# First heads of a pair kept unnormalized: one reciprocal row and one broadcast per pair instead of one per head

## The chip, the cores and the metric

The kernel runs on one core of one Trainium2 chip. TensorE (PE) multiplies matrices into PSUM, VectorE (DVE), ScalarE (ACT) and GpSimd (POOL) work element by element, and SyncE (SP) issues the DMAs here. Each engine has its own list of instructions and waits on semaphores for the others. The metric is device time in microseconds (us): the median of the timed runs, beside one profiled execution whose trace is read. Line numbers such as L390 are those of the kernel before, unless a text says otherwise.

## The reference

One block with two halves, on 2048 rows of 576 columns: attention over cached keys and values, then a gated MLP. Both are framed by a layer norm and by shift, gain and gate from a conditioning vector. Cut to what the change touches:

```python
q = (x @ wq).reshape(B, Sq, 32, 128).transpose(0, 2, 1, 3)
k = jnp.repeat(k_cache[:, :, Sk - 512:, :], 2, axis=1)     # 16 key/value heads, each used by two query heads
v = jnp.repeat(v_cache[:, :, Sk - 512:, :], 2, axis=1)
scores = jnp.einsum("bhqd,bhkd->bhqk", q, k) * (128 ** -0.5)
p = softmax(scores, axis=-1)
o = jnp.einsum("bhqk,bhkd->bhqd", p, v)
attn = o.transpose(0, 2, 1, 3).reshape(B, Sq, 4096) @ wo
x = x + ga * attn
...
x = x + gb * ((silu(h @ w1) * (h @ w3)) @ w2)
```

Here `h` is the normed, shifted and scaled `x`. The softmax divides each row of `p` by its sum. That division can be made on `p`, on `o`, or, as long as all heads that are added up share a row's factor, on the product with `wo`.

## The kernel before

The kernel works in 32-bit precision out of 16-bit matmuls: an operand is split into a high f16 part and the f16 rest, and three products (high x high, high x low, low x high) are added in PSUM. Nearly every tensor is therefore made twice: a copy or cast for the high part, and a subtraction for the low part.

The rows stand in four blocks of 512 columns. Attention goes through 128 **slots**. A slot is one query head on one block; slots come in **pairs**, the two query heads (j = 0 and j = 1) of one key/value head on one block. The order of all engines' instructions is the order in which the main loop (L1465 to L1511) writes them: no scheduler moves anything. A slot i has four steps, t = 0 to 3, one per 128 rows. In slot i stand, on the way of one head:

- `query(i+1)` (L375), steps 0 to 2: fourteen matmuls into `pq`, a PSUM bank of tag "A"; at step 2 ACT writes the high half of `qT` (L384), and at step 3 `query_low` (L390, DVE) the low half. That is the last read of `pq`.
- `scores(i, t)` (L392): three matmuls into `pss` (tag "S"); DVE takes the row maximum (L404) and scales it (L405). The third matmul is the only one that reads the low half of `qT`.
- `weights(i, t)` (L417, ACT): the exponential `p`, and its row sums into a column of `l`.
- `half_high` and `half_low` (L449 ACT, L454 POOL), and a DMA transpose (L461) turn `p` for steps 0 to 2; step 3 of the slot before is turned by PE (L440), with its halves by ACT (L444) and DVE (L469).
- `sums(i-1, step)`: the reciprocals of `l` (L424, DVE) at step 0, the store of this row of 512 numbers to DRAM (L427) at step 1, and at step 2 its load back to all 128 partitions as `r` (L430), 256 KB.
- `values(i-1)` (L471), at the end of the slot: twelve matmuls into `po`, again a bank of tag "A".
- `normalize(i-2)` (L484) at step 1: DVE multiplies `po` by `r` into `on`. `split_on(i-2)` (L494) at step 3: ACT casts `on` to the high half of `o` (L498), POOL makes the low half (L499).
- `attend_out` (L501): six matmuls per 128 rows and head into `pe` (L353). The pair's two heads are added up in PSUM, then DVE adds the sum, times a factor of the key/value head, to `acc` (L507).

Tag "A" has two banks in all. A new tile of a tag takes the bank that was released first, and its first writer waits for the last reader of that bank.

Around this, the slots carry other work at fixed steps: the splitting of keys, values and weights, and the preparation of the MLP's weights. The MLP stage then follows (`mlp`, L907) with PE matmuls of its own (L764, L849).

Of the kernel before, what the change touches and what calls it, by code (L numbers as in the profile page):

```python
# [9 lines left out]
F32 = mybir.dt.float32  # L10
F32R = mybir.dt.float32r
F16 = mybir.dt.float16
I32 = mybir.dt.int32
AF = mybir.ActivationFunctionType
ALU = mybir.AluOpType
# [4 lines left out]
P = 128  # L20
# [4 lines left out]
SB = 512  # L25
NSB = S // SB
ST = SB // P
# [5 lines left out]
HALF = D // 2  # L33
# [6 lines left out]
SCALE = float(DH) ** -0.5  # L40
P_LOG = 15 * math.log(2.0)
Q_DOWN = 2.0**-17
EXPONENT = 0x7F800000


@with_exitstack
def tile_block(
# [13 lines left out]
    nc = tc.nc  # L61
# [3 lines left out]
    pool = ctx.enter_context(tc.tile_pool(name="pool", bufs=2))  # L65
    odd = ctx.enter_context(tc.tile_pool(name="odd", bufs=2))
# [7 lines left out]
    def bank(tag, name):  # L74
        return psum.tile([P, 512], F32, tag=tag, name=name)


    E = psum.tile([P, 2, 512], F32, tag="E", name="pe", bufs=1)
# [6 lines left out]
    def half_split(a):  # L85
        return a.rearrange("p (a n) -> p a n", a=2)
# [139 lines left out]
    factors = const.tile([P, HKV, 3], F32, name="factors")  # L226
    peaks = {}

    def powers(small, ps, lo, hi, n, down):

        d, up = small[:, n + lo : n + hi], small[:, 2 * n + lo : 2 * n + hi]
        nc.vector.tensor_scalar(d.bitcast(I32), ps[:, lo:hi].bitcast(I32), EXPONENT, None, op0=ALU.bitwise_and)
        nc.vector.tensor_scalar(d, d, 2.0**-40, down, op0=ALU.max, op1=ALU.mult)
# [114 lines left out]
    def back(o, w, t, first, last):  # L348

        rows = slice(t * P, (t + 1) * P)  # L350
        for n, (x, y) in enumerate(((0, 0), (0, 1), (1, 0))):
            for h in range(2):
                nc.tensor.matmul(  # L353
                    E[:, h, :HALF],
                    o[:, x, rows],
                    w[:, y, h * HALF : (h + 1) * HALF],
                    start=first and n == 0,
                    stop=last and n == 2,
                )
# [6 lines left out]
    uses = [(g, (p, p + 1), p == 0) for p in (0, 2) for g in range(FIRST)]  # L366
    uses += [(g, tuple(range(NSB)), True) for g in range(FIRST, HKV - TAIL)]
    uses += [(g, (p, p + 1), p == 0) for p in (0, 2) for g in range(HKV - TAIL, HKV)]
    slots = [(u, j, b) for u, (_, blocks, _) in enumerate(uses) for b in blocks for j in range(2)]
    begins = [next(i for i, slot in enumerate(slots) if slot[0] == u) for u in range(len(uses))]  # L370
    n = len(slots)
    state = [dict() for _ in range(n)]
    hT, wqs, keys, vals, wos = {}, {}, {}, {}, {}

    def query(i, part):  # L375
# [6 lines left out]
        if part == len(QP) - 1:  # L382
            q = st["qT"] = pool.tile([P, 2, SB], F16, tag=("qh", "ql")[i % 2], name="qT", bufs=QB)
            nc.scalar.activation(q[:, 0], ps, AF.Copy, scale=Q_DOWN)  # L384
            if not i:
                query_low(i)

    def query_low(i):
        q, ps = state[i]["qT"], state[i].pop("q")
        nc.vector.scalar_tensor_tensor(q[:, 1], ps, Q_DOWN, q[:, 0], op0=ALU.mult, op1=ALU.subtract)  # L390

# [16 lines left out]
    def weights(i, t):  # L408

        u, j, b = slots[i]  # L410
        factor = factors[:, uses[u][0], j : j + 1]
        st = state[i]
        pss, nm = st.pop(("max", t))
        if t == 0:
            st["l"] = odd.tile([P, 2 * ST], F32, tag="l", name="l", bufs=3)
        p = pool.tile([P, SB], F32, tag="p", name="p", bufs=PB)
        nc.scalar.activation(p, pss, AF.Exp, bias=nm[:, 1:2], scale=factor, accum_out=st["l"][:, t : t + 1])  # L417
        st["p", t] = p

    def sums(i, step):  # L420

        st = state[i]
        if step == 0:
            nc.vector.reciprocal(st["l"][:, ST:], st["l"][:, :ST])  # L424
        elif step == 1:
            st["row"] = dram.tile([P, ST], F32, name=f"row{i}")
            nc.sync.dma_start(st["row"], st["l"][:, ST:])  # L427
        elif step == 2:
            st["r"] = pool.tile([P, P, ST], F32, tag="kv", name="r", bufs=8)
            nc.sync.dma_start(  # L430
                st["r"].rearrange("d p t -> d (p t)"), st["row"].rearrange("p t -> (p t)").partition_broadcast(P)
            )
# [38 lines left out]
    def values(i):  # L471
# [9 lines left out]
                )  # L481
        st["po"] = po

    def normalize(i):  # L484
        st = state[i]
        po = st.pop("po")
        on = st["on"] = pool.tile([P, SB], F32, tag="raw", name="on", bufs=RB)
        nc.vector.tensor_mul(
            on.rearrange("d (t p) -> d t p", t=ST),
            po.rearrange("d (t p) -> d t p", t=ST),  # L490
            st["r"].rearrange("d p t -> d t p"),
        )

    def split_on(i):  # L494
        st = state[i]
        on = st.pop("on")
        o = st["o"] = pool.tile([P, 2, SB], F16, tag=("ah", "al")[i % 2], name="o", bufs=3)
        nc.scalar.copy(o[:, 0, :], on)  # L498
        nc.gpsimd.tensor_sub(o[:, 1, :], on, o[:, 0, :])  # L499

    def attend_out(pair, t, j, total):  # L501
        u, _, b = slots[2 * pair]
        back(state[2 * pair + j]["o"], wos[u][:, j], t, j == 0, j == 1)
        if j == 1:
            run(*total)
            a = half_split(acc[b][:, t, :])
            nc.vector.scalar_tensor_tensor(  # L507
                a, E[:, :, :HALF], factors[:, uses[u][0], 2:3], a, op0=ALU.mult, op1=ALU.add
            )


# [457 lines left out]
    def run(i, t):  # L969
        for task, args in tasks.pop((i, t), ()):  # L970
            task(*args)
# [20 lines left out]
    def scale_cols(kind, ps, small, down):  # L992

        nc.tensor.matmul(ps[:, :P], ones, spreads.pop(kind)[:, :P], start=True, stop=True)
        nc.vector.tensor_reduce(small[:, 2:3], ps[:, :P], axis=AX.X, op=ALU.max)
        powers(small, small[:, 2:3], 0, 1, 5, down)
        for v in (vecs["shift", kind], vecs["gain", kind]):
            nc.vector.tensor_scalar(v, v, small[:, 10:11], None, op0=ALU.mult)

    def scale_first():  # L1000
# [3 lines left out]
        scale_cols("a", bank("S", "ps_top"), small, 2.0**-9)  # L1004
        nc.vector.tensor_scalar(score_down, small[:, 5:6], SCALE / Q_DOWN, None, op0=ALU.mult)

# [45 lines left out]
    def power_of(up, d, down):  # L1052

        nc.vector.tensor_scalar(d.bitcast(I32), d.bitcast(I32), EXPONENT, None, op0=ALU.bitwise_and)
        nc.vector.tensor_scalar(d, d, 2.0**-40, down, op0=ALU.max, op1=ALU.mult)
# [295 lines left out]
    for c in range(3):  # L1351
        i = 117 + 3 * c
# [112 lines left out]
    for i in range(n + 2):  # L1465
        run(i, -1)
        for t in range(ST):
# [9 lines left out]
            if 2 <= i <= n and t == 1:  # L1477
                normalize(i - 2)
# [4 lines left out]
            if i < n:  # L1483
                weights(i, t)
# [5 lines left out]
            if 1 <= i <= n and t < 2:  # L1490
                sums(i - 1, t)
            if 2 <= i <= n and t == 3:
                split_on(i - 2)
# [5 lines left out]
            for piece in outs.get((i, t), ()):  # L1499
                attend_out(*piece, (i, ("total", t)))  # L1500
# [3 lines left out]
            if 1 <= i <= n and t == 2:  # L1504
                sums(i - 1, t)
# [3 lines left out]
        if i == n:  # L1509
            normalize(n - 1)  # L1510
            split_on(n - 1)  # L1511
# [64 lines left out]
```

## Time and profile before

| what | value |
|---|---|
| median of 3 runs | 2786.5 us (2784.73 to 2787.59) |
| the profiled execution, its own time | 2786.65 us |
| its span, first to last instruction | 2784.8 us |
| mean granted TensorE clock | 0.996 |
| attention slots | 128, about 11.6 to 14 us each |
| r loads, row stores | 128 each |
| all DMA traffic | 463 MB |

A page of the profile lists the busy time of each engine, the chain of work that ended last, the costliest groups of instructions, and the DMA issues. A row of a group reads: line, engine, operation, output<-input, shapes, count, then busy us and the mean ns of one, then the idle time of the engine just before them and who ended it. A timeline row reads: start in us, duration, engine, line, operation; in square brackets the idle time before it and who ended it. PE's matmuls overlap, so a group of twelve starts each about 0.22 us after the one ahead. Waits that PE names are the ones that cost time where PE is busy throughout.

### The profile page before, as it was taken

The page shows a single profiled execution, that of the slowest core. Times are in us where ns is not written, and L with a number is a line of the kernel's source. Part 1 is how long each engine was busy: PE and PEld are TensorE (multiplying, and loading weights), DVE is VectorE, ACT ScalarE, POOL GpSimd, SP SyncE. Part 2 cuts the span into 40 slices and gives each one's busy share as a digit, 9 for nine tenths or more (in the row PEclk, how much of TensorE's full clock was granted, in tenths as well). Part 3 has the DMA queues.
Part 4 walks back from the last instruction along what each step waited for, and adds up shares of the span by engine and source line. Part 5 has one row for each costly group of instructions (what it writes and reads, how often), then busy time and mean ns, then how long its engine had stood idle before and what let it go on. Part 6 is the DMA issues. An engine that isn't in the chain of part 4 may idle for free.

```text
span 2784.8 us, 45011 instructions
## 1 busy us (share of the span) xinstructions
PE 2707.0 (97%) x15536; PEld 1535.3 (55%) x15536; DVE 2002.7 (72%) x3556; ACT 1624.1 (58%) x3022; POOL 1864.4 (67%) x1729
## 2 busy tenths in 40 slices
PE   6999999999999999999999999999999999999998
PEld 3455555555555555555555555555555555555555
DVE  7776788777788787887876657777766656566566
ACT  4686777777777877777677635544443333333332
POOL 3567788888788877777669637688774455333435
PEclk9999999999999999999999999999999999999999
DMA  5777888877777888878879945656643444333332
GB/s 162 177 168 187 189 186 185 179 178 187 169 181 172 187 200 186 212 181 205 194 185 220 233 125 169 195 165 199 206 152 103 160 123 127 104 102 112 105 110 77
DMA packets 594421, 463.27 MB, mean 166 GB/s; under 512 B 443152, under 2 KB 472976, under 8 KB 593424
## 3 DMA queue, kind: packets, MB, share of 16 engines
q1 hardware_dynamic: 593584, 460.39, 64.4%
q8 instruction: 122, 2.00, 0.3%
q14 instruction: 107, 0.88, 0.1%
q10 hardware_dynamic: 608, 0.00, 0.0%
HBM read 263.60 MB, written 95.99 MB: 129 GB/s over the span
## 4 chain that ended last, share of the span: by engine, by line
PE 50%; DVE 3%; DMA 1%; POOL 1%; issue 1%; ACT 0%; SPq 0%; DVEq 0%; POOLq 0%; ACTq 0%
PE py L764 15%; PE px L764 11%; PE pe L849 7%; PE pf L849 6%; PE pe L353 3%; PE po L479 2%; PE pss L400 2%; PE pq L342 2%; DMA row<-l 1%; DMA r<-row 0%; PE pt L440 0%; DVE acc L507 0%; DVE table L404 0%; PE pq L346 0%; POOL hp L454 0%
## 5 line engine op out<-in xcount | busy, mean ns | idle before, releaser
L454 POOL TENSOR_TENSOR hp<-p,hp 128x512 f16<-128x512 f32 x384 | 447.9, 1169 | 285.3 <-ACT hp L449 161.9
L417 ACT ACTIVATE p<-pss,table,factors 128x512 f32<-128x512 f32 x512 | 396.9, 775 | 362.0 <-DVE table L405 183.9
L764 PEld LDWEIGHTS <-wset 128*128 128x128 f16 x3528 | 345.7, 98 | 336.7 <-issue 4.0
L404 DVE TENSOR_REDUCE table<-pss 128x1 f32<-128x512 f32 x512 | 350.5, 685 | 211.8 <-PE pss L400 210.7
L764 PE MATMUL py<-hset,wset 128*128 128x512 f16 x2016 | 483.6, 380 | 0.0
L353 PE MATMUL pe<-o 128*128 128x288 f16 x3072 | 458.8, 286 | 14.6 <-DVE acc L507 12.5
L400 PE MATMUL pss<-k,qT 128*128 128x512 f16 x1536 | 417.3, 380 | 11.2 <-ACT p L417 9.2
L353 PEld LDWEIGHTS <-o 128*128 128x128 f16 x3072 | 300.4, 98 | 187.8 <-issue 20.9
L479 PE MATMUL po<-ptw,v 128*128 128x512 f16 x1536 | 358.2, 381 | 7.4 <-DVE ptw L469 5.6
L764 PE MATMUL px<-hset,wset 128*128 128x512 f16 x1512 | 361.5, 379 | 1.6 <-ACT p L417 1.6
L342 PE MATMUL pq<-hT,wq 128*128 128x512 f16 x1092 | 281.3, 380 | 1.1 <-DVE hT L211 1.1
L91 POOL TENSOR_TENSOR akv<-u,akv 128x512 f16<-128x512 f32 x141 | 164.8, 1178 | 174.6 <-ACT akv L90 166.8
L449 ACT CAST hp<-p 128x512 f16<-128x512 f32 x384 | 237.3, 618 | 12.9 <-POOL hT L213 0.4
L479 PEld LDWEIGHTS <-v 128*128 128x128 f16 x1536 | 150.9, 100 | 169.6 <-issue 16.8
L849 PEld LDWEIGHTS <-akv 128*128 128x128 f16 x1728 | 169.6, 98 | 93.6 <-issue 4.5
L400 PEld LDWEIGHTS <-qT 128*128 128x128 f16 x1536 | 150.4, 100 | 123.5 <-issue 12.6
L507 DVE SCALAR_TENSOR_TENSOR acc<-pe,factors,acc 128x576 f32<-128x576 f32 x256 | 207.7, 812 | 13.7 <-PE pe L353 10.4
L499 POOL TENSOR_TENSOR o<-on,o 128x512 f16<-128x512 f32 x128 | 150.2, 1173 | 55.8 <-ACT o L498 52.4
L342 PEld LDWEIGHTS <-wq 128*128 128x128 f16 x1104 | 108.6, 98 | 138.4 <-issue 9.0
L843 DVE SCALAR_TENSOR_TENSOR acc<-pf,table,acc 128x576 f32<-128x576 f32 x140 | 113.5, 811 | 80.6 <-PE pf L849 80.6
L944 ACT COPY u<-py 128x512 f32<-128x512 f32 x72 | 42.2, 586 | 200.5 <-PE py L764 198.6
L937 ACT ACTIVATE s<-s,table 128x512 f32<-128x512 f32 x72 | 52.0, 722 | 173.0 <-DVE s L936 173.0
(228 smaller groups left out, 4826.4 us busy)
## 6 DMA issues: line engine op xcount, KB each, us to landing
wset<-wd SPq DMA_DIRECT2D x213, 320.0 KB, 3.2
r<-row SPq DMA_DIRECT2D x128, 256.0 KB, 4.0
oset<-od SPq DMA_DIRECT2D x106, 288.0 KB, 3.2
wraw<-in_w SPq DMA_DIRECT2D x36, 768.0 KB, 5.5
wd<-wmade SPq DMA_DIRECT2D x75, 320.0 KB, 3.2
wset<-wd SPq DMA_DIRECT2D x71, 160.0 KB, 2.2
w2raw<-in_w SPq DMA_DIRECT2D x19, 576.0 KB, 4.9
wd<-ring SPq DMA_DIRECT2D x33, 320.0 KB, 2.8
```

The lines of the kernel that those rows point to most:

```text
L91: eng.tensor_sub(halves[:, 1], src, halves[:, 0])
L342: nc.tensor.matmul(ps, w[:, k // 2, m, :], hT[:, DC + m if k == 1 else m, :], start=s == 0, stop=False)
L353: nc.tensor.matmul(E[:, h, :HALF], o[:, x, rows], w[:, y, h * HALF : (h + 1) * HALF], start=first and n == 0, stop=last and n == 2,)
L400: nc.tensor.matmul(pss, q[:, x, rows], k[:, y, :], start=n == 0, stop=n == 2)
L404: nc.vector.tensor_reduce(nm[:, 0:1], pss, axis=AX.X, op=ALU.max, negate=True)
L417: nc.scalar.activation(p, pss, AF.Exp, bias=nm[:, 1:2], scale=factor, accum_out=st["l"][:, t : t + 1])
L449: nc.scalar.copy(hp[:, 0, :], state[i]["p", t])
L454: nc.gpsimd.tensor_sub(hp[:, 1, :], state[i].pop(("p", t)), hp[:, 0, :])
L479: nc.tensor.matmul(po, v[:, x, c, :], pt[:, y, c, :], start=c == 0 and n == 0, stop=c == KC - 1 and n == 2)
L507: nc.vector.scalar_tensor_tensor(a, E[:, :, :HALF], factors[:, uses[u][0], 2:3], a, op0=ALU.mult, op1=ALU.add)
L764: nc.tensor.matmul(ps, w[:, a, :], h[:, b, :], start=start and n == 0, stop=stop and n == 6, skip_group_check=True)
L849: nc.tensor.matmul(ps[:, h, :HALF], a[:, rows], w[:, b, :], start=m == 0, stop=m == 2)
```

## The change

The first head of a pair (j = 0) is no longer normalized. Its `po`, times a constant 2^-24, goes straight into the f16 halves of `o`: the high half by ACT at step 1 (`normalize`), the low half by DVE at step 3 (`split_on`), both out of PSUM. The second head (j = 1) is multiplied by the ratio of the first sum to the second (times 2^-24), so that both heads of a pair carry the same row factor. That factor, the first sum's reciprocal times the key/value head's factor, is applied where the pair's sum is added to `acc`; there rows stand on partitions, and the factor is a column of `l`. The tile `l` now holds both heads of a pair. Reciprocals, the stored row and its broadcast load are made for second heads only.

```diff
+O_DOWN = 2.0**-24
...
         if t == 0:
-            st["l"] = odd.tile([P, 2 * ST], F32, tag="l", name="l", bufs=3)
+            st["l"] = odd.tile([P, 6 * ST], F32, tag="l", name="l", bufs=4) if j == 0 else state[i - 1]["l"]
...
     def sums(i, step):
 
+        u, j, b = slots[i]
         st = state[i]
+        if j == 0:
+            return
+        first, both, up, ratio = (st["l"][:, lo * ST : hi * ST] for lo, hi in ((0, 1), (0, 2), (2, 4), (4, 5)))
         if step == 0:
-            nc.vector.reciprocal(st["l"][:, ST:], st["l"][:, :ST])
+            nc.vector.reciprocal(up, both)
+            nc.vector.scalar_tensor_tensor(ratio, first, O_DOWN, up[:, ST:], op0=ALU.mult, op1=ALU.mult)
         elif step == 1:
             st["row"] = dram.tile([P, ST], F32, name=f"row{i}")
-            nc.sync.dma_start(st["row"], st["l"][:, ST:])
+            nc.sync.dma_start(st["row"], ratio)
...
+    def new_o(i):
+        return pool.tile([P, 2, SB], F16, tag=("ah", "al")[i % 2], name="o", bufs=3)
+
     def normalize(i):
         st = state[i]
+        if slots[i][1] == 0:
+            o = st["o"] = new_o(i)
+            nc.scalar.activation(o[:, 0, :], st["po"], AF.Copy, scale=O_DOWN)
+            return
         po = st.pop("po")
...
     def split_on(i):
         st = state[i]
+        if slots[i][1] == 0:
+            o, po = st["o"], st.pop("po")
+            nc.vector.scalar_tensor_tensor(o[:, 1, :], po, O_DOWN, o[:, 0, :], op0=ALU.mult, op1=ALU.subtract)
+            return
         on = st.pop("on")
-        o = st["o"] = pool.tile([P, 2, SB], F16, tag=("ah", "al")[i % 2], name="o", bufs=3)
+        nc.vector.tensor_scalar(
+            st["l"][:, 5 * ST :], st["l"][:, 2 * ST : 3 * ST], factors[:, uses[slots[i][0]][0], 2:3], 1.0 / O_DOWN,
+            op0=ALU.mult, op1=ALU.mult,
+        )
+        o = st["o"] = new_o(i)
         nc.scalar.copy(o[:, 0, :], on)
         nc.gpsimd.tensor_sub(o[:, 1, :], on, o[:, 0, :])
...
-                a, E[:, :, :HALF], factors[:, uses[u][0], 2:3], a, op0=ALU.mult, op1=ALU.add
+                a, E[:, :, :HALF], state[2 * pair]["l"][:, 5 * ST + t : 5 * ST + t + 1], a, op0=ALU.mult, op1=ALU.add
```

Three places in the order of instructions, all in slot 80 (block and head alike in the middle of the attention stage; its po group starts at 1026.31 us in the trace before). Slot 80 is the first head of a pair, so `normalize` and `split_on` there treat head 78, a first head, and `values` treats head 79, a second head. In brackets stand the semaphores that an instruction waits for; Activation and DVE are those that the two engines count up. First PE, at the end of the slot, where `values(79)` opens its `po`; before:

```order
L353 MATMUL pe_76<-o_11090,o_11804 128x288
L479 LDWEIGHTS v_10634 [waits DMAHW5_49,DMAHW3_49]
L479 MATMUL po_11959<-ptw_11753,v_10634 128x512 [waits Activation_49]
L479 LDWEIGHTS v_10634
L479 MATMUL po_11959<-ptw_11753,v_10634 128x512
L479 LDWEIGHTS v_10634
L479 MATMUL po_11959<-ptw_11753,v_10634 128x512 [waits DVE_49]
```

and now (L479 has become L485):

```order
L354 MATMUL pe_76<-o_10867,o_11564 128x288
L485 LDWEIGHTS v_10419 [waits DMAHW6_49,DMAHW5_49,DMAHW3_49]
L485 MATMUL po_11718<-ptw_11514,v_10419 128x512 [waits DVE_49]
L485 LDWEIGHTS v_10419
L485 MATMUL po_11718<-ptw_11514,v_10419 128x512
L485 LDWEIGHTS v_10419
L485 MATMUL po_11718<-ptw_11514,v_10419 128x512
```

The DVE wait has moved from the third matmul to the first. Before, the count it waited for was that of L469 (the low half of the turned `p`); now it is that of `query_low` (L390, now L391), whose tile `pq` is the one whose bank this `po` takes. The first heads' groups keep the order of before.

Second, DVE in the same slot from the maximum of step 1 to the end of step 3; before:

```order
L404 TENSOR_REDUCE table<-pss 128x1
L405 TENSOR_SCALAR table<-table,factors 128x1
L488 TENSOR_TENSOR on<-po,r 128x512
L507 SCALAR_TENSOR_TENSOR acc_88<-pe,factors,acc_88 128x576
L241 TENSOR_REDUCE us<-kvraw 128x1
L404 TENSOR_REDUCE table<-pss 128x1
L405 TENSOR_SCALAR table<-table,factors 128x1
L469 TENSOR_TENSOR ptw<-pt,ptw 128x4x128
L404 TENSOR_REDUCE table<-pss 128x1
L405 TENSOR_SCALAR table<-table,factors 128x1
L390 SCALAR_TENSOR_TENSOR qT<-pq,qT 128x512
L507 SCALAR_TENSOR_TENSOR acc_89<-pe,factors,acc_89 128x576
```

and now:

```order
L405 TENSOR_REDUCE table<-pss 128x1
L406 TENSOR_SCALAR table<-table,factors 128x1
L528 SCALAR_TENSOR_TENSOR acc_88<-pe,l,acc_88 128x576
L242 TENSOR_REDUCE us<-kvraw 128x1
L405 TENSOR_REDUCE table<-pss 128x1
L406 TENSOR_SCALAR table<-table,factors 128x1
L475 TENSOR_TENSOR ptw<-pt,ptw 128x4x128
L405 TENSOR_REDUCE table<-pss 128x1
L406 TENSOR_SCALAR table<-table,factors 128x1
L391 SCALAR_TENSOR_TENSOR qT<-pq,qT 128x512
L511 SCALAR_TENSOR_TENSOR o<-po,o 128x512
L528 SCALAR_TENSOR_TENSOR acc_89<-pe,l,acc_89 128x576
```

The multiplication L488 of step 1 is gone, and the second read of `po`, the low half of `o` (L511), stands at step 3 behind `query_low`.

Third, ACT over the same steps, from the first exponential of the slot; before:

```order
L417 ACTIVATE p,l<-pss,table,factors 128x512
L449 CAST hp<-p 128x512
L417 ACTIVATE p,l<-pss,table,factors 128x512
L449 CAST hp<-p 128x512
L444 CAST ptw<-pt 128x4x128
L417 ACTIVATE p,l<-pss,table,factors 128x512
L449 CAST hp<-p 128x512
L384 ACTIVATE qT<-pq 128x512
L417 ACTIVATE p,l<-pss,table,factors 128x512
L498 CAST o<-on 128x512
```

and now:

```order
L418 ACTIVATE p,l<-pss,table,factors 128x512
L455 CAST hp<-p 128x512
L497 ACTIVATE o<-po 128x512
L418 ACTIVATE p,l<-pss,table,factors 128x512
L455 CAST hp<-p 128x512
L450 CAST ptw<-pt 128x4x128
L418 ACTIVATE p,l<-pss,table,factors 128x512
L455 CAST hp<-p 128x512
L385 ACTIVATE qT<-pq 128x512
L418 ACTIVATE p,l<-pss,table,factors 128x512
```

The high half of `o` has moved from step 3 (L498, behind the last exponential) to step 1 (L497, ahead of the second), and so ahead of `qT`.

More of the change, by code (lines that the diff above doesn't have):

```diff
@@ L414, in weights @@
         if t == 0:
-            st["l"] = odd.tile([P, 2 * ST], F32, tag="l", name="l", bufs=3)
+            st["l"] = odd.tile([P, 6 * ST], F32, tag="l", name="l", bufs=4) if j == 0 else state[i - 1]["l"]
         p = pool.tile([P, SB], F32, tag="p", name="p", bufs=PB)
-        nc.scalar.activation(p, pss, AF.Exp, bias=nm[:, 1:2], scale=factor, accum_out=st["l"][:, t : t + 1])
+        nc.scalar.activation(p, pss, AF.Exp, bias=nm[:, 1:2], scale=factor, accum_out=st["l"][:, j * ST + t : j * ST + t + 1])
         st["p", t] = p
     def sums(i, step):
+        u, j, b = slots[i]
         st = state[i]
+        if j == 0:
+            return
+        first, both, up, ratio = (st["l"][:, lo * ST : hi * ST] for lo, hi in ((0, 1), (0, 2), (2, 4), (4, 5)))
         if step == 0:
-            nc.vector.reciprocal(st["l"][:, ST:], st["l"][:, :ST])
+            nc.vector.reciprocal(up, both)
+            nc.vector.scalar_tensor_tensor(ratio, first, O_DOWN, up[:, ST:], op0=ALU.mult, op1=ALU.mult)
         elif step == 1:
             st["row"] = dram.tile([P, ST], F32, name=f"row{i}")
-            nc.sync.dma_start(st["row"], st["l"][:, ST:])
+            nc.sync.dma_start(st["row"], ratio)
         elif step == 2:
```

## The prediction

> **What bounds the kernel now.** I read the page's busy shares and its chain first, then the time in three stages, then who TensorE (PE) waits for in the attention stage, and last the timeline of single slots.
>
> ```profile
> PE 2707.0 (97%) x15536; PEld 1535.3 (55%) x15536; DVE 2002.7 (72%) x3556; ACT 1624.1 (58%) x3022; POOL 1864.4 (67%) x1729
> ...
> 100.00:1500.00 1400.00, 1380.49 (x7971) 784.17 (x7969) 1097.63 (x2216) 1069.40 (x2069) 1098.83 (x1045) 1.00 0.81 186
> 1500.00:1620.00 120.00, 111.03 (x637) 62.63 (x636) 71.41 (x134) 71.92 (x140) 76.79 (x68) 1.00 0.93 225
> ...
> PE pe L353 <- DVE acc L507: 5.6, 8, 1.3
> PE pss L400 <- ACT p L417: 5.6, 8, 1.7
> PE po L479 <- DVE ptw L469: 2.0, 6, 0.5
> ```
>
> PE is the bound: in the attention stage (100 to 1500 us, second row, whose columns are the stretch, its length and the busy time of PE, PEld, DVE, ACT and POOL, then PE's granted clock) it is busy for 1380.5 of 1400 us. Only 19.5 us are idle there. The last three rows, the waits of PE in that stretch (total, times, longest), name 13 of them. So whatever the change takes off DVE, POOL, ACT or the queues can earn at most these 19.5 us and a part of the 9 us idle between 1500 and 1620. What makes PE wait anew is lost in full. The question is therefore which instruction PE waits for after the change that it did not wait for before.
>
> **What the change takes away and adds, off PE.**
>
> ```profile
> L488 DVE TENSOR_TENSOR on<-po,r 128x512 f32<-128x512 f32 x128 | 138.9, 1085 | 16.8 <-POOL o L499 8.4 <-DMA r<-row 6.1 <-PE po L479 1.8
> L390 DVE SCALAR_TENSOR_TENSOR qT<-pq,qT 128x512 f16<-128x512 f32 x127 | 87.6, 690 | 63.5 <-ACT qT L384 63.0
> L424 DVE RECIPROCAL l<-l 128x4 f32<-128x4 f32 x128 | 21.5, 168 | 2.4 <-ACT p L417 2.1 <-issue 0.2
> L405 DVE TENSOR_SCALAR table<-table,factors 128x1 f32<-128x1 f32 x512 | 109.6, 214 | 18.2
> L233 DVE TENSOR_SCALAR us<-us 128x4 f32<-128x4 f32 x15 | 11.3, 752 | 0.5
> L384 ACT ACTIVATE qT<-pq 128x512 f16<-128x512 f32 x127 | 75.1, 591 | 0.6 <-PE pq L346 0.6
> L498 ACT CAST o<-on 128x512 f16<-128x512 f32 x128 | 78.1, 610 | 7.1 <-DVE on L488 7.1
> L499 POOL TENSOR_TENSOR o<-on,o 128x512 f16<-128x512 f32 x128 | 150.2, 1173 | 55.8 <-ACT o L498 52.4
> ...
> r<-row SPq DMA_DIRECT2D x128, 256.0 KB, 4.0
> row<-l SPq DMA_DIRECT2D x128, 2.0 KB, 2.8
> ```
>
> Half of each of these 128 goes, since there are 64 first heads: on POOL 64 x 1.173 = 75 us, on the queue 64 row stores and 64 loads of 256 KB. DVE loses 64 x (1.085 + 0.168) = 80 us. It gains 64 low halves of o, which have the form of L390 (PSUM in, f16 out, 0.69 us: 44 us), 64 ratios of 128x4, and 64 products of 128x4. No row shows a 128x4 scalar_tensor_tensor; the bounds are 0.17 (L424) and 0.75 us (L233), and I take 0.21 (L405, two scalars too). For the 128x4 tensor_scalar I take 0.65, near L233, which is the same operation and size; the ends are 0.21 and 0.75. So DVE's total hardly moves (-80 + 44 + 13 + 42 = +19 us). ACT swaps an SBUF cast (0.61) for a PSUM copy (L384's form, 0.59), but two steps earlier in the slot. All this is beside PE, and would earn nothing by itself. The wider reciprocal and the per-tile scale of L507 (another 128x1 column) I cost at nothing.
>
> **The new wait.** Tag A of PSUM has two banks, used by pq of the next slot and by po in turn. Before, po(i-2) was read out by L488 at step 1, so po(i-1) found that bank long free; pq(i+1) kept the other. Now a first head's po is read a second time, by the low half at step 3, which stands on DVE right behind query_low (L390). So when values(i-1) opens its po, the bank that is freed first is that of pq(i+1), and L390 frees it. In the order of instructions, 63 of the 128 po groups (all second heads' but the last) have this wait on their first matmul, and none had it before.
>
> How late is L390 when PE wants to begin those po groups? The timeline of one slot:
>
> ```profile
> 1024.93 0.81 PE L400 MATMUL pss<-k,qT 128*128 128x512 f16 x3
> 1025.26 0.78 ACT L417 ACTIVATE p<-pss,table,factors 128x512 f32<-128x512 f32 x1 [1.15 <-DVE table L405]
> 1025.58 0.90 PE L353 MATMUL pe<-o 128*128 128x288 f16 x6
> 1025.78 0.69 DVE L404 TENSOR_REDUCE table<-pss 128x1 f32<-128x512 f32 x1
> 1026.16 0.62 ACT L449 CAST hp<-p 128x512 f16<-128x512 f32 x1
> 1026.31 2.75 PE L479 MATMUL po<-ptw,v 128*128 128x512 f16 x12
> 1026.50 0.22 DVE L405 TENSOR_SCALAR table<-table,factors 128x1 f32<-128x1 f32 x1
> 1026.69 0.59 ACT L384 ACTIVATE qT<-pq 128x512 f16<-128x512 f32 x1
> 1027.31 0.69 DVE L390 SCALAR_TENSOR_TENSOR qT<-pq,qT 128x512 f16<-128x512 f32 x1 [0.59 <-ACT qT L384]
> 1028.90 0.81 PE L400 MATMUL pss<-k,qT 128*128 128x512 f16 x3
> ```
>
> PE begins po at 1026.31; L390 ends at 1028.00. Before, that cost nothing: only the third score matmul after 1028.90 needs it. Now PE stands 1.69 us. The same difference, taken from the 63 pairs of such rows in the whole trace, of which these are the first, a long one and the last:
>
> ```profile
> 80.88 0.59 PE L479 MATMUL po<-ptw,v 128*128 128x512 f16 x2
> 83.57 0.69 DVE L390 SCALAR_TENSOR_TENSOR qT<-pq,qT 128x512 f16<-128x512 f32 x1 [0.70 <-ACT qT L384]
> ...
> 714.51 2.80 PE L479 MATMUL po<-ptw,v 128*128 128x512 f16 x12
> 716.90 0.69 DVE L390 SCALAR_TENSOR_TENSOR qT<-pq,qT 128x512 f16<-128x512 f32 x1 [1.11 <-ACT qT L384]
> ...
> 1583.94 2.75 PE L479 MATMUL po<-ptw,v 128*128 128x512 f16 x12
> 1584.36 0.69 DVE L390 SCALAR_TENSOR_TENSOR qT<-pq,qT 128x512 f16<-128x512 f32 x1
> ```
>
> is 3.38, 3.08 and 1.11 us there, never under 0.71, 1.87 in the mean, 118 us in sum. It can't go to nothing: L390 stands on DVE behind the maximum of the slot's last scores, so after those end (1025.74 above) come 0.69 + 0.22 + 0.69 = 1.60 us of DVE, while PE has only the six matmuls of L353 until 1026.31. That leaves 1.03 us per pair, 65 us in all, even with every queue empty.
>
> **What shifts the 118 us.** (1) ACT's copy of the high half now stands before p of step 1, ahead of qT. In 23 of the 63 slots ACT has no gap of 0.25 us on the way from there to qT, and L390 waits for qT; counted slot by slot, the 0.6 us adds 13 us (bounds: none, and 63 x 0.6 = 38). (2) L488 is gone from step 1 of these slots. This helps only where L507 behind it ran late (22 slots; elsewhere L507 waits for PE anyway), and where p waited for DVE: -7 us (bounds 0 and 63 x 1.085 = -68). (3) The product of 0.65 us at step 3 of the slot before delays DVE's first maximum; it was already over 0.5 us late in 36 of the slots, and in 19 ACT then runs gapless up to qT. I add 10 us (0 to 36 x 0.75 = 27). (4) While PE stands, DVE, ACT and POOL work on and start the next slots with less arrears. Between none and all of what exceeds the floor (118 - 65 = 53), I take half: -27 us. (5) Some of PE's old waits fall into the new ones: of 19.5 + 9 us I take -8.
>
> (6) The clock. Long stands can lower it:
>
> ```profile
> 92.28 0.81 PE L400 MATMUL pss<-k,qT 128*128 128x512 f16 x3 [2.48 <-ACT p L417]
> ...
> 93.80:97.20 3.40, 3.30 (x9) 1.10 (x8) 1.79 (x4) 3.34 (x8) 1.99 (x3) 0.51 1.08 385
> ...
> 1572.79 2.32 PE L479 MATMUL po<-ptw,v 128*128 128x512 f16 x10 [2.92 <-DVE ptw L469]
> ...
> 1573.00:1576.00 3.00, 3.00 (x15) 1.35 (x14) 2.17 (x5) 2.97 (x7) 2.23 (x2) 1.00 0.06 19
> ```
>
> After a wait of 2.48 us the granted clock is 0.51 for 3.4 us (1.7 us of work lost); after one of 2.92 it stays 1.00. With (1) to (3), 23 of my 63 stands exceed 2.3 us. One in two of these at 1.7 us gives +20 us (bounds 0, and 39 if each one does).
>
> [...]
>
> **Sum.** 118 + 13 - 7 + 10 - 27 - 8 + 20 = 119 us, all in the stretch from 66 to 1590 us; the MLP stage behind it has the same PE order and no new wait. The profiled execution took 2786.65 us (span 2784.8), the median of the three runs is 2786.5, so the sum is made against either: 2786.6 + 119 = 2906 us.
>
> **Rivals.** (A) The stands fall to the floor, because the stalled PE lets all arrears go: 65 us less 8 of old waits, 2844 us. For it: most arrears are worked off within one slot, and 19 of the 63 differences are already below 1.3. Against: the long ones come from work inside their own slot, as in the slot of 714.51, where ACT is busy without a gap from its first p on. Chance 0.12. (B) The stands don't shrink (27 us more) and each long one lowers the clock (19 more): 2952 us. For it: the 2.48 us above. Chance 0.12. (C) Not slower: PE finds a bank free after all, since L390 comes before po. It decides at 1.03 us per pair: ACT's qT and the last maximum would have to come that much earlier. Then only the relief is left, about the 5.6 us of waits for L507 and half as much again from the end of the stage: 2778 us. Against it stands the floor, which no lighter queue moves. Chance 0.04. That leaves 0.72 for the forecast, which I'd put between 2860 and 2945.
>
> **Range and chances.** 2850 to 2955 leaves out (A) and (C). About 0.2% (5.6 us) is what a measurement of this kernel can tell from no change. (C) splits evenly: faster 0.02, within 0.2% 0.02, slower 0.96.
>
> **What would show it.** In the profile after, the waits of PE should hold a new first row, po waiting for DVE qT (query_low), some 63 times, 1 to 3.5 us each, 80 to 140 us in total; PE's busy share falls to 93% at the same PE work, and the L390 row follows a shorter wait of the score matmuls. If that row is there at about 65 us, (A) is right; if the clock row shows many stretches at half, (B). A row of waits for the low half of o, or for row and r, would be a wait I have not seen; no such row and no longer span would be (C).

## The result and the profile after

| what | before | after |
|---|---|---|
| median | 2785.82 us (4 runs) | 2918.14 us (4 runs, 2915.25 to 2921.87) |
| ratio, 95% interval | | 1.0475 (1.0457 to 1.0493) |
| the profiled execution, its span | 2786.65, 2784.8 us | 2921.87, 2920.1 us |
| PE busy | 2707.0 us | 2738.2 us |
| PE idle (span less busy) | 77.8 us | 181.9 us |

The changed kernel is slower by 132 us; 119 were forecast, with a range of 2850 to 2955 us. In the profiled executions the span grew by 135.3 us: 104.1 of PE idle, and 31.2 of PE busy with the same 15536 matmuls. The profiled execution of the changed kernel took 3.7 us more than its median, which the sums against its trace contain. The two parts are taken in turn. First the page's busy times, its row of the matmuls of `po` with the idle time ahead of them, and the loads of `r`; under them, from the table of PE's waits over the whole span, four that concern the slots (total, times, longest); then the same rows of the kernel before:

```profile
PE 2738.2 (94%) x15536; PEld 1544.0 (53%) x15536; DVE 2017.8 (69%) x3620; ACT 1623.1 (56%) x3022; POOL 1792.7 (61%) x1665
...
L485 PE MATMUL po<-ptw,v 128*128 128x512 f16 x1536 | 381.3, 400 | 118.6 <-DVE qT L391 113.9
...
r<-row SPq DMA_DIRECT2D x64, 256.0 KB, 3.8
```

```profile
PE po L485 <- DVE qT L391: 113.9, 63, 3.1
PE pss L401 <- ACT p L418: 12.5, 13, 2.4
...
PE pe L354 <- DVE acc L528: 5.1, 6, 1.6
...
PE po L485 <- DVE ptw L475: 4.2, 3, 3.0
```

```profile
L479 PE MATMUL po<-ptw,v 128*128 128x512 f16 x1536 | 358.2, 381 | 7.4 <-DVE ptw L469 5.6
...
PE pe L353 <- DVE acc L507: 12.5, 15, 1.7
...
PE pss L400 <- ACT p L417: 9.2, 10, 2.5
PE po L479 <- DVE ptw L469: 5.6, 8, 2.9
```

The first wait of the changed kernel did not exist before: 63 waits of `po` for `query_low`, 1.81 us in the mean. Such a wait, in which PE does nothing, is called a stand here. The row alone exceeds the growth of PE's idle time by 9.8 us; by so much PE's other idle time shrank, most of all its wait for `acc` (12.5 to 5.1 us). What the change takes off the other engines is there too (POOL from 1864.4 to 1792.7 us, half the loads), and earns little beside the new wait.

The stretch of 1170 us that ends the program, first of the kernel before and then of the changed one (stretch, length, busy of PE, PEld, DVE, ACT, POOL, PE's granted clock, DMA share, GB/s), shows that the MLP has no part in it:

```profile
1615.00:2785.00 1170.00, 1152.30 (x6678) 654.53 (x6676) 764.80 (x1052) 429.39 (x719) 645.37 (x567) 0.99 0.43 136
```

```profile
1750.00:2920.00 1170.00, 1152.77 (x6680) 654.88 (x6678) 766.10 (x1054) 429.15 (x719) 645.24 (x567) 1.00 0.43 136
```

One new wait in the changed kernel's timeline (start, duration, engine, line, operation, idle time before and its releaser), and under it windows around two other stands, which are taken up further down, and around this one (last two rows):

```profile
1080.53 0.90 PE L354 MATMUL pe<-o 128*128 128x288 f16 x6
...
1081.26 0.50 PE L1065 MATMUL pe<-table 128*128 128x2 f32 x4
...
1082.12 0.59 ACT L385 ACTIVATE qT<-pq 128x512 f16<-128x512 f32 x1
...
1082.75 0.69 DVE L391 SCALAR_TENSOR_TENSOR qT<-pq,qT 128x512 f16<-128x512 f32 x1 [0.95 <-ACT qT L385]
...
1083.36 0.68 DVE L511 SCALAR_TENSOR_TENSOR o<-po,o 128x512 f16<-128x512 f32 x1
...
1083.49 4.44 PE L485 MATMUL po<-ptw,v 128*128 128x512 f16 x12 [1.73 <-DVE qT L391]
```

```profile
346.87:350.28 3.41, 0.80 (x7) 0.49 (x5) 1.89 (x4) 3.38 (x7) 3.41 (x4) 1.00 0.24 73
350.28:353.70 3.42, 3.06 (x8) 1.14 (x8) 2.77 (x4) 3.01 (x6) 3.26 (x4) 0.50 0.40 77
766.71:770.12 3.41, 1.54 (x9) 0.87 (x9) 1.50 (x3) 3.35 (x8) 3.33 (x5) 1.00 0.68 183
770.12:773.53 3.41, 1.59 (x8) 0.75 (x8) 2.33 (x4) 3.41 (x7) 3.25 (x4) 1.00 0.40 78
773.53:776.95 3.42, 3.42 (x20) 1.75 (x19) 1.74 (x3) 1.66 (x3) 3.34 (x4) 1.00 0.10 21
1080.73:1084.15 3.42, 1.69 (x14) 1.17 (x13) 2.44 (x6) 3.39 (x9) 3.34 (x4) 1.00 0.89 218
1084.15:1087.56 3.41, 3.41 (x10) 1.21 (x9) 2.16 (x6) 0.65 (x1) 3.25 (x4) 0.50 1.18 181
```

PE has nothing left at 1081.76 (1081.26 + 0.50), the copy of `qT` on ACT and `query_low` on DVE follow each other, and `po` opens 0.05 us after `query_low` ends at 1083.44. That is the wait. The group of twelve then takes 4.44 us; in the prediction's slot of the kernel before it took 2.75. The last window says why: the granted clock there is 0.50. That is the second part of the loss. Between 100 and 1600 us the clock is at half for 54.6 us in 14 stretches, which are 16 windows of 3.41 us; term (6) counted half of 23 stands, about 12. In the kernel before the clock is never at half there.

### The profile page after: what moved, and what is told of

Same layout as the page of the kernel before. It is cut to its first block, busy times and chain, and to the rows that moved or that the text cites. A ratio compares the mean times of both kernels' runs of the same rounds, so it can differ in the third digit from the quotient of the medians.

```text
span 2920.1 us, 44717 instructions
## 1 busy us (share of the span) xinstructions
PE 2738.2 (94%) x15536; PEld 1544.0 (53%) x15536; DVE 2017.8 (69%) x3620; ACT 1623.1 (56%) x3022; POOL 1792.7 (61%) x1665
## 4 chain that ended last, share of the span: by engine, by line
PE 70%; DVE 11%; ACT 8%; issue 3%; POOL 1%; ACTq 0%; DVEq 0%; POOLq 0%
PE py L785 15%; PE px L785 11%; PE po L485 10%; PE pe L354 7%; PE pq L343 7%; PE pe L870 6%; PE pss L401 6%; PE pf L870 6%; DVE table L405 2%; ACT p L418 2%; ACT hp L455 2%; DVE qT L391 2%; DVE acc L528 2%; PE pt L446 1%; ACT qT L385 1%
## 5 line engine op out<-in xcount | busy, mean ns | idle before, releaser
L485 PE MATMUL po<-ptw,v 128*128 128x512 f16 x1536 | 381.3, 400 | 118.6 <-DVE qT L391 113.9
L401 PE MATMUL pss<-k,qT 128*128 128x512 f16 x1536 | 417.9, 381 | 13.3 <-ACT p L418 12.5
L485 PEld LDWEIGHTS <-v 128*128 128x128 f16 x1536 | 157.6, 104 | 304.9 <-issue 165.3
L528 DVE SCALAR_TENSOR_TENSOR acc<-pe,l,acc 128x576 f32<-128x576 f32 x256 | 207.7, 811 | 57.1 <-PE pe L354 45.3
L401 PEld LDWEIGHTS <-qT 128*128 128x128 f16 x1536 | 151.3, 100 | 124.6 <-issue 20.5
L864 DVE SCALAR_TENSOR_TENSOR acc<-pe,table,acc 128x576 f32<-128x576 f32 x140 | 113.1, 808 | 35.2 <-PE pe L870 35.2
```

The costliest lines, as they stand in the source:

```text
L401: nc.tensor.matmul(pss, q[:, x, rows], k[:, y, :], start=n == 0, stop=n == 2)
L485: nc.tensor.matmul(po, v[:, x, c, :], pt[:, y, c, :], start=c == 0 and n == 0, stop=c == KC - 1 and n == 2)
L528: nc.vector.scalar_tensor_tensor(a, E[:, :, :HALF], state[2 * pair]["l"][:, 5 * ST + t : 5 * ST + t + 1], a, op0=ALU.mult, op1=ALU.add)
L864: nc.vector.scalar_tensor_tensor(into, ps[:, :, :HALF], factor, into, op0=ALU.mult, op1=ALU.add)
```

## Experiments

Each kernel is compared with runs of the kernel before made beside it, whose medians lie between 2786.57 and 2788.24 us. "The row" is PE's wait of `po` for the bank, whoever releases it.

### Only the bank is held longer

The kernel before, whose first heads' multiplication by `r` moves from step 1 to step 3, behind `query_low`. Nothing else of the change is in it.

```diff
-            if 2 <= i <= n and t == 1:
+            if 2 <= i <= n and t == 1 and slots[i - 2][1]:
                 normalize(i - 2)
...
                 query_low(i + 1)
+            if 2 <= i <= n and t == 3 and not slots[i - 2][1]:
+                normalize(i - 2)
```

> The kernel before, with one thing moved: the multiplication of first heads by r stands at step 3 behind query_low instead of at step 1, so that their po bank is held as long as in the change. Nothing else of the change is in it. Theory 'bank' (the loss is PE's wait for the bank that query_low frees, and the clock that falls in it): 63 new waits of po for DVE qT, 105 to 125 us in total, 10 to 30 us of half clock, 2890 to 2930 us. Rival 'work' (the loss comes from the small DVE instructions and the copy that ACT makes earlier): at most 2795 us.

Measured: 2899.87 us, ratio 1.0408 (1.0393 to 1.0424). The page's busy times and PE's first wait:

```profile
PE 2724.7 (94%) x15536; PEld 1539.6 (53%) x15536; DVE 2004.7 (69%) x3556; ACT 1632.5 (56%) x3022; POOL 1865.9 (64%) x1729
```

```profile
PE po L479 <- DVE qT L390: 108.3, 63, 3.1
```

The same row, the same 63 times, and 113 us of the 132. No ratio, no product, no different eviction is needed for it: what costs is where the last read of the first head's `po` stands. The edit also moves 1.09 us of DVE's work to step 3, but PE's waits for `p` (7.6 us) and `acc` (4.9) are no longer than before.

### The same low half, read earlier

The changed kernel, with the first heads' low half at the end of step 2 instead of step 3, so ahead of `query_low`.

```diff
-            if 2 <= i <= n and t == 3:
+            if 2 <= i <= n and t == 3 - (slots[i - 2][1] == 0):
                 split_on(i - 2)
```

> The changed kernel, with the low half of first heads' o made at step 2 instead of step 3, ahead of query_low. All its added work stays. Theory 'bank': po takes the bank of the first head's po again, the 63 waits for DVE qT vanish, at most 0.3 us of waiting for the low half is left in each slot, no half clock in the attention stage; 2775 to 2800 us. Rival 'work': still above 2890 us.

Measured: 2802.95 us, ratio 1.0061 (1.0044 to 1.0078), 3 us above what was expected. The row has another releaser, the low half itself:

```profile
PE po L485 <- DVE o L511: 18.8, 24, 1.5
```

One step earlier takes 115 us off the changed kernel. Even so the low half is the last thing PE waits for in 24 of the pairs, for up to 1.5 us where at most 0.3 was expected.

In between stands the low half at step 3, right ahead of `query_low`.

```diff
+            if 2 <= i <= n and t == 3 and slots[i - 2][1] == 0:
+                split_on(i - 2)
             if t == 3 and i + 1 < n:
                 query_low(i + 1)
...
-            if 2 <= i <= n and t == 3:
+            if 2 <= i <= n and t == 3 and slots[i - 2][1]:
                 split_on(i - 2)
```

> The changed kernel, with the low half at step 3 but right ahead of query_low on DVE, so that po waits for the low half, which stands behind the last maximum but does not wait for ACT's qT. Theory 'bank' with the floor of the prediction (1.03 us of DVE behind the last scores): 63 waits of 0.9 to 1.5 us, 60 to 85 us, nearly no half clock, 2845 to 2875 us; what lies between this and the change is ACT being late with qT. If instead the arrears of DVE itself made the long waits, they stay near 114 us and the time near 2918.

Measured: 2873.76 us, ratio 1.0313 (1.0298 to 1.0328).

```profile
PE po L485 <- DVE o L511: 75.7, 58, 3.0
PE po L485 <- ACT qT L385: 5.0, 3, 2.4
```

So changing places with one instruction gives 44 us. In the profiles the row falls by 33 (113.9 to 80.7; the sum of both rows here) and PE's busy time by 17 (2738.2 to 2720.9). The slot that stood 1.73 us above, now:

```profile
1047.61 0.21 DVE L406 TENSOR_SCALAR table<-table,factors 128x1 f32<-128x1 f32 x1
1047.74 0.68 DVE L511 SCALAR_TENSOR_TENSOR o<-po,o 128x512 f16<-128x512 f32 x1
1048.15 0.59 ACT L385 ACTIVATE qT<-pq 128x512 f16<-128x512 f32 x1
...
1048.48 2.76 PE L485 MATMUL po<-ptw,v 128*128 128x512 f16 x12 [0.69 <-DVE o L511]
1048.77 0.69 DVE L391 SCALAR_TENSOR_TENSOR qT<-pq,qT 128x512 f16<-128x512 f32 x1 [0.35 <-ACT qT L385]
```

The low half takes the place on DVE that `query_low` had and is as long; what it doesn't need is ACT's copy of `qT`. In 41 of the 63 pairs of the changed kernel DVE sat idle for that copy ahead of `query_low`, 28.1 us in all (0.95 in this slot). Laid pair by pair, PE's waits fall by 30.5 us in these 41 and by 0.9 in the other 22. So what lies between the two kernels' waits is ACT being late with `qT`, as was expected. The other expectation, waits of 0.9 to 1.5 us, missed: 21 are longer, up to 3.0. In these 21 DVE begins the slot's last maximum 1.15 us in the mean after the scores' end, in the other 42 after 0.16. So DVE's arrears make the long waits that are left.

### The side terms: where ACT's copy stands, and the small product

The changed kernel, with the first heads' high half at step 2 behind the query copy on ACT:

```diff
-            if 2 <= i <= n and t == 1:
+            if 2 <= i <= n and t == 1 and slots[i - 2][1]:
                 normalize(i - 2)
...
             if i + 1 < n and t < ST - 1:
                 query(i + 1, t)
+            if 2 <= i <= n and t == 2 and slots[i - 2][1] == 0:
+                normalize(i - 2)
```

> The changed kernel, with ACT's high half of first heads at step 2 behind qT instead of at step 1 ahead of it. The wait for query_low stays. By term (1) of the prediction, 13 us of waits go (0.6 us in some 23 slots): 2890 to 2912 us, waits for qT about 95 to 105 us. If the copy's place does not matter, it stays within 6 us of 2918.

Measured: 2905.0 us, ratio 1.0427 (1.0412 to 1.0443); 13 us less than the changed kernel, as term (1) had it, but not by the way it had it:

```profile
PE po L485 <- DVE qT L391: 110.0, 62, 3.1
PE pss L401 <- ACT p L418: 8.3, 8, 1.9
```

The row fell by only 3.9 us, to 110.0 where 95 to 105 were expected. Another 4.2 came from the scores' wait for `p`, and PE's busy time fell by 6.1 (2738.2 to 2732.1), about half of the 13.6 us by which the time at half clock fell.

The changed kernel, with the 128x4 product on POOL:

```diff
-        nc.vector.tensor_scalar(
+        nc.gpsimd.tensor_scalar(
             st["l"][:, 5 * ST :], st["l"][:, 2 * ST : 3 * ST], factors[:, uses[slots[i][0]][0], 2:3], 1.0 / O_DOWN,
```

> The changed kernel, with the 128x4 product of second heads (the factor column) on POOL instead of DVE. By term (3) of the prediction, about 10 us of waits go (its 0.35 us in the profile after is half of what was assumed, so 4 to 10 us): 2906 to 2916 us. If DVE's arrears at the start of the slots do not reach qT, it stays within 6 us of 2918.

Measured: 2906.71 us, ratio 1.0426 (1.0411 to 1.044); 11 us less. The page's busy times and the row:

```profile
PE 2726.3 (94%) x15536; PEld 1541.3 (53%) x15536; DVE 1998.3 (69%) x3556; ACT 1624.6 (56%) x3022; POOL 1809.5 (62%) x1729
```

```profile
PE po L485 <- DVE qT L391: 111.1, 62, 3.1
```

The row is 2.8 us shorter. PE's busy time fell by 11.9 (2738.2 to 2726.3), the time at half clock between 100 and 1600 us from 54.6 to 30.7. In this pair of profiles most of the gain is clock. Such a split is read from one profiled execution of each kernel; the granted clock of the four runs with this edit goes from 0.985 to 0.990 at times within 2 us of each other, so the split can't be taken to a few us.

Both edits together, with nothing else changed:

> The changed kernel with two of its side terms taken away together: ScalarE's high half goes to step 2 behind the query copy (alone: 2905.0 us, 13 us less), and the 128x4 product goes to GpSimd (alone: 2906.7 us, 11 us less). The low half stays where the change has it, so the bank is held as long. If the two terms are separate delays they add up: 2890 to 2898 us, no more than 10 us from the run that only holds the bank (2899.9 us), and the row of waits for the query copy falls to 104 to 109 us. Rival: both act through the same thing, the clock that falls when the stands come in the wrong place, and one of them alone already gives it back: 2903 us or more, with the row still near 110 us.

Measured: 2900.7 us, ratio 1.0411 (1.0395 to 1.0427); the two edits give 17 us, not the 24 of their sum.

```profile
PE po L485 <- DVE qT L391: 106.4, 62, 3.1
```

The row fell by 7.5 us, about the 3.9 and 2.8 together, and into the first theory's range. The time at half clock is 41.0 us in this profile, no less than with ACT's edit alone. That would fit waits that add up and a clock that doesn't, but it isn't shown: each of these ratios is known to 4 or 5 us either way, so the 7 us that are missing from the sum aren't clear of the noise, and the time lies between the two theories' ranges. What is left (2900.7) is about what the held bank alone costs (2899.87).

### Work in the stand

The changed kernel, with five more matmuls of 512 columns ahead of each second head's `po` group, into a bank that nothing reads.

```diff
+        if 1 <= i < n - 1 and slots[i - 1][1]:
+            ps, q, k = t_bank(), state[i]["qT"], keys[slots[i][0]]
+            for m in range(5):
+                nc.tensor.matmul(ps, q[:, 0, :P], k[:, 0, :], start=True, stop=True)
         if 1 <= i <= n:
             values(i - 1)
```

> The changed kernel with five more 512-column matmuls (1.08 us, into a bank that nobody reads) ahead of the po group of each second head, so in the stretch where PE stands. The wait for query_low stays. If half clock in the stands costs what the profile's clock says (some 28 us of PE work), the stands shrink to about 45 to 55 us, half-clock stretches in the attention stage nearly vanish, PE busy is about 2775 us, and the kernel gets faster with more work: 2885 to 2902 us. If the clock costs nothing, the time is 2918 us or, with the short stands overfilled, 2918 to 2925 us.

Measured: 2894.01 us, ratio 1.0379 (1.0363 to 1.0395): 315 more matmuls, and 24 us less than the changed kernel. The page's busy times and PE's first wait:

```profile
PE 2777.4 (96%) x15851; PEld 1565.6 (54%) x15851; DVE 2018.4 (70%) x3620; ACT 1623.2 (56%) x3022; POOL 1792.7 (62%) x1665
```

```profile
PE po L485 <- DVE qT L391: 48.9, 47, 2.0
```

At 0.22 us each (twelve in 2.75 us) the 315 take about 69 us at full clock, by estimate; PE's busy time grew by 39.2. So some 30 us of the matmuls' time came back. There is no stretch at half clock between 100 and 1600 us any more. `query_low` is as late as it was: from the end of the work ahead of the five matmuls to its end it is 111.8 us over the 63 pairs, and 110.5 in the changed kernel. PE just had work in that time, and its clock was not at half (54.6 us in the changed kernel).

### The bank released early on purpose

The changed kernel with both halves early: ACT's at step 0, DVE's at step 1, where L488 stood.

```diff
-            if 2 <= i <= n and t == 1:
+            if 2 <= i <= n and t == slots[i - 2][1]:
                 normalize(i - 2)
+            if 2 <= i <= n and t == 1 and slots[i - 2][1] == 0:
+                split_on(i - 2)
...
-            if 2 <= i <= n and t == 3:
+            if 2 <= i <= n and t == 3 and slots[i - 2][1]:
                 split_on(i - 2)
```

> The changed kernel with both reads of a first head's po early: ACT's high half at step 0, ahead of the first exponential, and DVE's low half at step 1, where the multiplication L488 stood. Theory 'bank': no wait of po for a bank is left, PE busy is back at 2707 us, and the relief of the rest of the change shows by itself: 2772 to 2788 us. Rival: if the change's added instructions cost time of their own, it stays at 2800 us or more, as with the low half at step 2.

Measured: 2778.12 us, ratio 0.9962 (0.995 to 0.9975): faster than both kernels, by 10 us (0.4%) than the one before. PE's longest waits in attention:

```profile
PE pss L401 <- ACT p L418: 10.1, 10, 2.5
...
PE po L485 <- DVE ptw L475: 6.1, 10, 3.0
PE pe L354 <- DVE acc L528: 6.0, 9, 1.6
```

No row names a bank. The wait for `acc` (12.5 us in 15 waits before) has halved: 6.5 of the 7.7 us by which the profiled span is below that of the kernel before. That is the relief that rival (C) counted, and the time is (C)'s 2778 us, once the wait of the change is gone. Which part of the lighter queues brings it was not tried alone.

With the low half at step 2, but ahead of that step's scores:

```diff
+            if 2 <= i <= n and t == 2 and slots[i - 2][1] == 0:
+                split_on(i - 2)
             if i < n:
                 scores(i, t)
...
-            if 2 <= i <= n and t == 3:
+            if 2 <= i <= n and t == 3 and slots[i - 2][1]:
                 split_on(i - 2)
```

> The changed kernel with the low half on DVE at step 2 ahead of the maximum of that step (one place ahead of the run with the low half at step 2, which left 18.8 us of waits for it). Theory 'bank': those waits fall to under 3 us, 2782 to 2792 us. If instead the low half there delays the maximum, p and qT by as much, it stays at 2800 us.

Measured: 2786.8 us, ratio 0.9995 (0.9987 to 1.0004): no difference from before, as the theory of the bank had it. The row is gone here too, but the scores' wait for `p` is 14.9 us in 14 waits (9.2 in 10 before). That fits a reader that leaves the bank free in time but now stands ahead of the maximum on DVE; the place of ACT's copy differs between these two versions too, so it isn't shown which of them matters.

Last the fast version (both halves early) with the 128x4 product on POOL, by the edit shown above for it:

> The changed kernel with both halves of the first head's eviction in the next slot's first two steps, as in the run that beat both kernels (2778.1 us), and the 128x4 product of the denominators moved from VectorE to GpSimd. If VectorE's queue at step 3 still delays the softmax (the pss row of that run, 10.1 us in 10 waits) and the adds of the output projection (6.0 us in 9), the 353 ns taken off VectorE 64 times (23 us of its time) shorten those two rows: 2768 to 2775 us. Rival: with no bank held, nothing waits for VectorE's step-3 queue, and GpSimd's product only moves: 2776 to 2782 us, no difference that five pairs can tell. A VectorE total near 1998 us and a PE busy time near 2706 us belong to both.

Measured: 2772.21 us, ratio 0.9952 (0.994 to 0.9965). PE's waits that answer to the three rows of the version without it:

```profile
PE pss L401 <- ACT p L418: 8.3, 6, 2.5
PE po L485 <- DVE ptw L475: 6.4, 10, 3.0
PE pe L354 <- DVE acc L528: 5.3, 7, 1.6
```

The rows of the scores and of `acc` are shorter, by 2.5 us together, as the first theory had it, and the time is in its range. The intervals of the two fast versions overlap, so that the product's share is not shown; that this version beats both kernels is.

### All runs side by side

The time over before is the profiled span less 2784.8 us; half clock is the total between 100 and 1600 us; more PE busy is against 2707.0 us. Each row is one profiled execution.

| kernel | over before | the row | half clock | more PE busy |
|---|---|---|---|---|
| changed | 135.3 | 113.9 | 54.6 | 31.2 |
| bank held alone | 110.3 | 108.3 | 34.1 | 17.7 |
| low half right ahead of `query_low` | 86.4 | 80.7 | 20.5 | 13.9 |
| high half behind the query copy | 121.3 | 110.0 | 41.0 | 25.1 |
| product on POOL | 119.0 | 111.1 | 30.7 | 19.3 |
| both of these | 117.2 | 106.4 | 41.0 | 23.0 |
| low half at step 2 | 16.1 | 18.8 | 6.8 | -0.8 |
| extra matmuls | 110.5 | 48.9 | 0 | 70.4 |
| both halves early | -7.7 | none | 3.4 | -1.0 |
| low half at step 2, ahead of the scores | -0.9 | none | 6.8 | -3.0 |
| both halves early, product on POOL | -14.4 | none | 3.4 | -3.1 |

In each of the first eight rows the wait and the additional busy time together exceed the time over before by 2 to 16 us; by so much PE's other idle time shrank. In the first seven, the additional busy time is half of the time at half clock, to within 5 us.

## Why the prediction was right, and where it was off

**The wait.** "All second heads' but the last", 63 waits on `query_low`, 1 to 3.5 us each, 80 to 140 in total: 63 times, 0.78 to 3.1, 113.9 us. The differences of 118 us that were read off the trace of before, pair by pair, go with the 63 measured waits at a correlation of 0.85. The run that only holds the bank shows that this wait is the change's cost, and the runs that read the low half earlier show that it hangs on the place of that one read. Its length has two sources, both named in the prediction: DVE's work at the slot's end, and in 41 pairs ACT being late with `qT`.

**Rival (A)**, the floor of 65 us, is not what came: the row stayed at 1.81 us per pair. Nor are the 1.03 us a floor: they were read off one slot, in 13 of the 63 pairs the wait is shorter (0.78 to 0.96 us), and the prediction's own smallest difference was 0.71. **Rival (C)** fell with the 63 waits. **Rival (B)** had one half right: the row is 20 us below the 134 of stands that don't shrink, yet the clock was at half in more places than the forecast counted.

**Terms (1) to (5)** made, with the 118, 99 us of idle time (118 + 13 - 7 + 10 - 27 - 8); measured are 104.1. That the sum is so close is in part luck, as the single terms show:

(1) ACT's copy at step 1, +13: the edit that moves it gave 13 us. That the size agrees is luck, since the route was wrong: 3.9 in the new wait, the rest through the scores' wait for `p` and the clock.

(2) L488 gone, -7: not tried alone.

(3) The product, +10: the edit gave 11 us, though the product took 353 ns and not the 650 that were taken for it. Its way into the row is 2.8 us; most of the 11 is clock, as far as one profile of each can tell. So here too the size was right by luck.

(4) Arrears worked off, -27: taking the other terms as forecast, the row of 113.9 leaves -20 (118 + 13 - 7 + 10 = 134).

(5) Old waits absorbed, -8: 9.8.

**Term (6), the clock, was the mis-sized one:** +20 forecast, 31.2 us more PE busy measured, of which half of the 54.6 us at half clock is 27. It counted stands over 2.3 us (23 forecast, 15 came) at one in two. The trace shows that the length of one stand doesn't decide. (A window is here a stretch of 3.41 us on the grid on which the recorded changes of the clock lie.) Two stands of 2.97 us: the one from 347.67 to 350.63 lies almost all in the window from 346.87 to 350.28, in which PE is busy for 0.80 us, and the next window has clock 0.50. The one from 768.98 to 771.94 is split between two windows, busy 1.54 and 1.59 us, and the third still has 1.00. And the stand of 1.73 us at 1081.76 was followed by half clock; it lies in one window with four matmuls of two columns.

The stretches at half clock between 100 and 1600 us start on a grid of 3.413 us (those at 350.28 and 1084.15 us lie 215 such steps apart). Thirteen last one window, 3.41 us, and one, from 1135.35, lasts three, 10.24 us. No new stand was longer than 3.1 us, so none filled a window, and yet 54.6 us were spent at half clock; the window from 346.87 was followed by it with PE busy for 0.80 us.

**The other engines.** DVE's total was forecast at +19 us and came at +15.1 (2002.7 to 2017.8). The groups of the operations that the trace of before did not have:

```profile
L511 DVE SCALAR_TENSOR_TENSOR o<-po,o 128x512 f16<-128x512 f32 x64 | 43.5, 680 | 0.0
...
L430 DVE SCALAR_TENSOR_TENSOR l<-l 128x4 f32<-128x4 f32 x64 | 25.7, 401 | 2.2
L514 DVE TENSOR_SCALAR l<-l,factors 128x4 f32<-128x4 f32 x64 | 22.6, 353 | 0.0
L497 ACT ACTIVATE o<-po 128x512 f16<-128x512 f32 x64 | 37.5, 586 | 0.0
```

The two large forms were taken from rows of their shape (0.69 and 0.59 us) and fit. The two small ones were between rows and missed, 401 ns for 210 and 353 for 650; over 64 of each these errors are +12 and -19 us, and partly cancel. "PE's busy share falls to 93% at the same PE work": it fell to 94%, and the busy time was not the same. The "shorter wait of the score matmuls" did not come: their idle time went from 11.2 to 13.3 us.

## What to carry to other kernels

A buffer that two stages share is released by its last reader, so when a change adds or moves a reader, ask first which instruction now stands last, and who waits for the bank next; here that was worth 113 us. Moving that one reader one step earlier took 115 us off, and moving both readers into the first two steps turned a loss of 132 us into a gain of 10. The pairwise difference between the new releaser's end and the waiter's start in the old trace was a good forecast of this wait. When the bound engine is made to stand many times, add the clock: here 63 stands of 0.78 to 3.1 us came with 54.6 us at half clock. Count it by windows and not by gaps: of the 15 windows of 3.41 us in which the changed kernel's PE was busy for less than 1.4 us, 13 were followed by half clock.

## What was not expected of the hardware

In these traces half clock goes with PE's busy time in a window of 3.41 us, not with the length of one stand. Laid over the twelve profiles of this case from 100 to 1600 us, a grid of 3.413 us that goes through a recorded drop gives 5203 windows that were not at half clock already. In 63 of them PE was busy for less than 1.4 us (41%); 61 of these were followed by half clock, and the two that weren't had 1.37 and 1.39. In the changed kernel alone these are 423 windows, 15 with less than 1.4 us, 13 of them followed by half clock. (The 1.4 was chosen from these same windows.) Of the 5140 others, 6 were followed by half clock: one with 1.40, and five, with 1.49 to 1.78, which all contain matmuls of one or two columns, as in the window of 1080.73 above (1.69 us, of which 0.50 are L1065's). Without those matmuls' time the five hold 1.15 to 1.44 us. Whether the narrow matmuls have a part in this was not tried.

The 128x4 product took 353 ns on DVE in the changed kernel. With it on POOL, POOL's busy time is 16.8 us higher (1792.7 to 1809.5) in 64 more instructions, so about 0.26 us each, by estimate, though POOL is the slower engine for the large forms here (1.17 us for the 128x512 subtraction of L499, against 0.68 on DVE for that of L469, which reads PSUM).
